# A layer norm moved to ScalarE, wider stores, eleven gather slots and a re-written order in a state-space and expert-lookup kernel

## The chip, the cores and the metric

The kernel runs on one core of one Trainium2 chip. The metric is the device time of one execution in microseconds; a verdict compares medians of several executions of the kernel before and the kernel after.

## What is computed

The reference takes 2048 tokens of 448 channels, normalises each token, and adds three things: the token itself, a long convolution along the sequence (branch A), and a lookup of experts (branch B).

```python
x = A_u
xn = _layernorm(x, axis=-1)
return x + _A_ref(xn, ...) + _B_ref(xn, ...)

# A: a state-space convolution per channel d, 256 states n, 2048 lags l
P = jnp.exp(logdA[:, :, None] * l[None, None, :])        # complex
K = jnp.einsum("dn,dnl,dn->dl", Cc, P, dB).real
y = irfft(rfft(pad(u)) * rfft(pad(K)))[:L] + u * Dskip

# B: 16 heads, best of 64 x 64 experts by two argmaxes
s1 = jnp.einsum("nhd,ed->nhe", q1, k1)
s2 = jnp.einsum("nhd,ed->nhe", q2, k2)
act = _gelu(jnp.einsum("nd,nhkd->nhk", xf, u[top_e]))
out = jnp.einsum("nhk,nhk,nhkd->nd", g, act, v[top_e])
```

## The kernel before

The work is written as some 3,400 small steps in 77 streams. Each step has an engine, a function that issues its instructions, the steps it depends on, and the buffers that it takes and gives back. A string, `ORDER`, holds one character for each step; the loop in `Plan.run` walks it and issues the steps. The order in which instructions stand on each engine is therefore fixed by that string; the costs that stand in the `p.add` calls are only notes of the program that wrote it and act on nothing. Synchronisation follows from the buffers: an instruction waits by a semaphore for the last reader or writer of what it touches. Each engine takes its instructions strictly in order, and so does the queue of loads and stores that SyncE issues (SP). The kernel also gives GpSimd (POOL) a queue of its own for gathers and for stores that add to memory.

The steps that the change and the prediction touch are these.

- **Layer norm** (`ln`, L895 on). Sixteen tiles `xx` of 128 tokens are loaded (L892) and normalised in pairs. VectorE (DVE) makes mean and variance of a tile with `bn_stats` (L909) and `bn_aggr` (L913), then ten small instructions a pair for the inverse root (L915 to L921), and ScalarE (ACT) applies scale and bias (L925) into the second half of the tile's buffer. The normalised tile goes to memory (`xn_d`, L929), to the transform of branch A (`up`, L724) and to the scores of branch B.
- **Scores** (`score`). TensorE (PE) multiplies the turned tile `xt` by combined weights `W` (L961, L970); DVE finds the maxima (L985, L992 and on). `W` is made at the start from the query weights `wq` (L855) and the keys (`wc`, L862) by PE and ACT.
- **Experts** (`experts`, L1062 on). For each tile of 128 tokens sixteen times: an indirect DMA on POOL gathers 128 rows of 3584 bytes into a slot `ue` (L1083), DVE takes the dot product of the first half of each row with the token's row `xr` (L1091, loaded at L1075), ACT and DVE make the weight, and PE adds up the second halves (`po`, L1121). PE's matmul gives four slots back. A finished tile is added to the output in memory by a POOL store with accumulation (L1136).
- **Convolution kernels** (`batch`, `products`). In 56 batches ACT makes exponentials and sines, DVE multiplies them (L660 to L666), PE turns them into the spectrum `VK` (L682, L702).
- **Convolution** (`conv`). The 448 channels go in chunks of 128, 128, 128 and 64. In each, four quarters are multiplied with the spectra (`U`, `cp`), turned back (`ip`, L825 and L830) and copied by ACT to `tq`. A store then puts `tq` to memory (`t_d`, L842) as rows of 128 (in the last chunk 64) numbers.
- **Last transform** (`final`). The stored quarters come back with another partition order (`tl`, L1166), PE multiplies them with the matrix `h` (L1178). In the first three chunks ACT copies the result and POOL adds it to the output in memory (L1192). The last chunk is written differently: `h` is loaded whole (`hb`, L1150), the output so far is read back into `bb` (L1156), DVE adds the two (L1182), and SP stores the sum (L1190).
- **Buffers**. One pool of 1024-number buffers holds the tiles `xx`, `W`, the gathered rows and most of the convolution's work. `OPT` gives 8 of them to gathered rows at the start; others join when the tiles, `W` and constants are used up.

Of the kernel before, what the change touches and what calls it, by code (L numbers as in the profile page):

```python
# [25 lines left out]
M = 2 * NB  # L26
# [89 lines left out]
class Plan:  # L116
# [57 lines left out]
    "44H444HH1HH2704HH7HH2HHH46HH7HH24444I6H4444H47H8CH22NI2H4241DE4HHC88142OC78D4D127H4H1EKECH74C44FLKF4CHHDL47HDEEFKDFFL24H"  # L174
    "27EC4J42HMF2HDC227KLI272223QEI47DC44E4346CDFFDK441C4QE4C9FDE978L88FDRQ9M4CREE94J74497J75RCKF5F8LQ4KCD977R71D4wE77E9778CL"
    "FFDEDAE6YFF7AYK9QHHLQANH7OQRHR9GR8S8AH9wQZH9HRaTwRHAQGHeRQYTHRQTHGQTRTRYHNHRHOSTQJTAQGMTHTeTHbQTRTTReTQUcQdQRVeNfRIVOWgg"
    "PXRQRfQPPPxBRRggHSxQTfgRxTyHeTRggIRZxTgwMXJxQKTyxHLyyfgQKLgzxQRh!!HRNRyyOz#xSPyyHQgzT!MH#QQxxggzgJTT$h!RyhTxRxR#HQRgfhgT"
    "#HQyTbghyh$yzQx!fHz!#NxyReOyiQ#TeHTHx$gyxRwYHeyxRTwxzQeUKHSeVQR!whgLhHwRjgHgcQQKQx!PRydzgY#yHRLHTbyIJRINHR#ThgThHx$bhHhH"
    "TOgKcLkRHVaTyMSdxgzxgT!!QiHxQzRyKHxQj#eHTyPTQRTyTHhxQfyTz!Hk#H%LggRRz$JhQMxH!iHjRRfhHRgxKg#TLHkyIfYhygTW#exyeTSexiX$KLYg"
    "lxKlLNMeyjzO!IHQzHgxKy!mygLPK#yTkTMxmQ#Hyl$ggwJQRHhzLRh!Thgmg!HezQfxhRex#gK#eQHwRwxThheHyxLgRgHR$y%QfggRHNxxOUiyjwfyzQ!z"  # L180
    "TMx!hy#byZSQggVVT#cQeHxyHRykHlgHHgzx$a!hRxJHgQ!gQHzTIYmhKTy&x#gLTh#digXIKTeQRyRTLJYP$fNjggTRhRlxOgeHyyHkHQzfKgh!gLxmzHHh"
# [21 lines left out]


class Kernel:
    OPT = dict(UE=8, XX=4, CS=2, ZI=2, MG=4, KT=4, HL=2, SG=1, XR=4, OB=3, XT=1, ST=1)
# [180 lines left out]
    def params(s, part):  # L387
# [874 lines left out]
```

## Time and profile before

| what | value |
|---|---|
| time before, median of 3 runs | 782.04 us (777.7 to 784.82) |
| the profiled execution, its own time | 777.9 us |
| its span, from first to last instruction | 776.1 us |
| mean granted TensorE clock | 0.908 |
| DVE busy | 680.7 us (88%) |
| PE busy | 658.5 us (85%) |
| ACT busy | 535.7 us (69%) |
| POOL busy | 351.3 us (45%) |
| moved by DMA | 212.36 MB, mean 274 GB/s |

The profile is of one execution. Busy time is the time in which an engine had an instruction running; shares are of the span. Views that group instructions give the count, the busy time and the mean of one instruction, then the idle time ahead of them and what ended it. A view by windows gives, for each stretch of time, busy time by engine, the clock granted to TensorE, the share of the 16 DMA engines that was busy, and GB/s.

### The profile page before, as it was taken

The page shows a single profiled execution, that of the slowest core. Times are in us where ns is not written, and L with a number is a line of the kernel's source. Part 1 is how long each engine was busy: PE and PEld are TensorE (multiplying, and loading weights), DVE is VectorE, ACT ScalarE, POOL GpSimd, SP SyncE. Part 2 cuts the span into 40 slices and gives each one's busy share as a digit, 9 for nine tenths or more (in the row PEclk, how much of TensorE's full clock was granted, in tenths as well). Part 3 has the DMA queues.
Part 4 walks back from the last instruction along what each step waited for, and adds up shares of the span by engine and source line. Part 5 has one row for each costly group of instructions (what it writes and reads, how often), then busy time and mean ns, then how long its engine had stood idle before and what let it go on. Part 6 is the DMA issues. An engine that isn't in the chain of part 4 may idle for free.

```text
span 776.1 us, 19859 instructions
## 1 busy us (share of the span) xinstructions
PE 658.5 (85%) x7628; PEld 358.9 (46%) x7628; DVE 680.7 (88%) x1727; ACT 535.7 (69%) x1071; POOL 351.3 (45%) x303
## 2 busy tenths in 40 slices
PE   1999999998999998999888967788995775899982
PEld 0434343443434344434356644456763442577751
DVE  5878659998999999999999999799998999999840
ACT  1756237457677597665668899698797998789720
POOL 2011033353623435557455474555466585744620
PEclk9999999999999999999899997566996767699995
DMA  9997956767867859778999999898898997999996
GB/s 310 355 331 287 318 163 209 261 197 243 273 205 222 260 174 310 235 239 265 319 338 329 314 345 306 271 254 269 257 315 286 348 302 237 345 296 293 274 264 125
DMA packets 139975, 212.36 MB, mean 274 GB/s; under 512 B 45096, under 2 KB 121896, under 8 KB 139816
## 3 DMA queue, kind: packets, MB, share of 16 engines
q0 software_dynamic: 29120, 124.27, 50.2%
q1 hardware_dynamic: 110760, 86.81, 36.8%
q8 instruction: 60, 0.98, 0.5%
q14 instruction: 35, 0.29, 0.1%
HBM read 181.42 MB, written 33.29 MB: 277 GB/s over the span
## 4 chain that ended last, share of the span: by engine, by line
DVE 30%; PE 29%; DMA 19%; ACT 12%; issue 7%; POOL 1%; SPq 1%; DVEq 0%; ACTq 0%; POOLq 0%
PE sc L961 10%; DMA ue<-in_uv_dram,ig 7%; DVE ue L1091 7%; DVE zi L662 3%; DVE ph L614 3%; DVE mg L666 3%; DMA xr<-xn_d 3%; PE wc L862 3%; PE kp L682 2%; PE sc L970 2%; ACT CS L629 2%; PE ip L830 2%; ACT CS L632 2%; DVE cp L808 2%; PE up L724 2%
## 5 line engine op out<-in xcount | busy, mean ns | idle before, releaser
L1083 POOL DMA_INDIRECT ue<-in_uv_dram,ig x256 | 307.3, 1200 | 334.4 <-PE po L1121 87.1
L961 PE MATMUL sc<-W,xt 128*128 128x512 f32 x384 | 181.4, 612 | 4.6 <-ACT xt L946 3.8
L1091 DVE SCALAR_TENSOR_TENSOR ue<-ue,xr 128x448 f32<-128x448 f32 x256 | 155.8, 619 | 17.4 <-DMA ue<-in_uv_dram,ig 11.6
L961 PEld LDWEIGHTS sc<-W,xt 128*128 128x128 f32 x384 | 69.7, 192 | 93.8 <-issue 82.7
L1121 PE MATMUL po<-ue,A 128*32 128x448 f32 x512 | 70.1, 616 | 10.2 <-issue 3.9
L682 PE MATMUL kp<-mg 128*32 128x64 f32 x1792 | 64.1, 240 | 14.9 <-DVE mg L666 6.5
L590 ACT ACTIVATE mg<-lg 128x512 f32<-128x512 f32 x112 | 63.2, 597 | 18.7 <-PE lg L579 17.9
L629 ACT ACTIVATE CS<-ph 128x1024 f32<-128x1024 int32 x56 | 62.7, 1120 | 8.0 <-DVE ph L614 5.4
L662 DVE TENSOR_TENSOR zi<-mg,CS 128x1024 f32<-128x1024 f32 x56 | 68.2, 1218 | 0.0
L666 DVE TENSOR_TENSOR mg<-mg,CS 128x1024 f32<-128x1024 f32 x56 | 68.2, 1217 | 0.0
L614 DVE CUSTOM_DVE_ANT_0 ph<-st,ph 128x512 uint16<-128x512 uint16 (+2 forms) x84 | 65.1, 775 | 0.3
L635 ACT ACTIVATE CS<-CS,halfpi 128x1024 f32<-128x1024 f32 x56 | 64.4, 1151 | 0.5
L682 PE MATMUL kp<-zi 128*32 128x64 f32 x1792 | 63.4, 238 | 0.0
L632 ACT ACTIVATE CS<-ph 128x1024 f32<-128x1024 int32 x56 | 63.1, 1127 | 0.1
L682 PEld LDWEIGHTS kp<-mg 128*32 128x32 f32 x1792 | 46.5, 121 | 35.3 <-issue 8.6
L702 PE MATMUL vp<-f,kt 128*64 128x128 f32 x448 | 42.0, 319 | 21.9 <-DVE kt L693 9.3
L985 DVE TENSOR_REDUCE mx<-sc 128x8 f32<-128x512 f32 x64 | 43.7, 683 | 14.5 <-PE sc L970 10.8
L579 PE MATMUL lg<-lc,rt 32*128 32x512 f32 x112 | 40.4, 564 | 14.4 <-ACT mg L590 10.8
L682 PEld LDWEIGHTS kp<-zi 128*32 128x32 f32 x1792 | 48.8, 123 | 0.1
L702 PEld LDWEIGHTS vp<-f,kt 128*64 128x64 f32 x448 | 27.8, 156 | 45.3 <-DVE kt L693 9.0
L798 PE MATMUL U<-VU,g 128*64 128x128 f32 x384 | 42.2, 299 | 5.4 <-DVE cp L808 3.4
L830 PE MATMUL ip<-cp,e 64*128 64x256 f32 x384 | 45.4, 383 | 0.2 <-ACT tq L837 0.2
(246 smaller groups left out, 1221.3 us busy)
## 6 DMA issues: line engine op xcount, KB each, us to landing
wq<-in_wq_dram SPq DMA_DIRECT2D x32, 448.0 KB
xr<-xn_d SPq DMA_DIRECT2D x64, 224.0 KB
vu_d<-vst SPq DMA_DIRECT2D x64, 112.0 KB
VU<-vu_d SPq DMA_DIRECT2D x12, 512.0 KB
t_d<-tq SPq DMA_DIRECT2D x24, 256.0 KB
tl<-t_d SPq DMA_DIRECT2D x12, 512.0 KB
ue<-in_uv_dram,ig POOLq DMA_INDIRECT x256, 6.4
xx<-in_x_dram SPq DMA_DIRECT2D x16, 224.0 KB
```

The costliest lines, as they stand in the source:

```text
L614: s.nc.vector.tensor_tensor(out=rw(n, 2 * n), in0=rw(0, n), in1=o["st"][:, k, b0:b0 + 2].rearrange("p b h m x -> p (b h m x)")[:, None].to ...
L629: s.nc.scalar.activation(CS[:, 1].rearrange("p (m r x) -> p m r x", r=16, x=2), four(s.ph), AF.Sin, scale=SC)
L632: s.nc.scalar.activation(B["CS"][:, 0].rearrange("p (m r x) -> p m r x", r=16, x=2), four(s.ph), AF.Abs)
L635: s.nc.scalar.activation(B["CS"][:, 0], B["CS"][:, 0], AF.Sin, scale=-SC, bias=s.halfpi)
L662: V.tensor_tensor(out=zi[:, 512:], in0=mg[:, 512:], in1=CS[:, 1], op=ALU.mult)
L666: V.tensor_tensor(out=mg[:, 512:], in0=mg[:, 512:], in1=CS[:, 0], op=ALU.mult)
L682: s.nc.tensor.matmul(kp[32 * c:32 * c + 32, 64 * gi:64 * gi + 64], T[ri][:, 1024 + m:1056 + m], view(T[ri], m, [[512, 2], [1, 32]]), start ...
L702: s.nc.tensor.matmul(vp[64 * ri:64 * ri + 64, 128 * gi:128 * gi + 128], B["kt"][:, 64 * gi:64 * gi + 64], s.f1[:, ri], start=True, stop=True)
L961: s.nc.tensor.matmul(B["sc", q].rearrange("p a b -> p (a b)"), B["xt"][:, i], w, start=(q % 2 == 0 and i == 0), stop=(q % 2 == 1 and i == 2))
L1083: s.nc.gpsimd.indirect_dma_start(out=ue, out_offset=None, in_=s.io["uv"], in_offset=bass.IndirectOffsetOnAxis(ap=s.IDX[t][:, c, g:g + 1].b ...
L1091: s.nc.vector.scalar_tensor_tensor(Q["ue", c][:, :D], Q["ue", c][:, :D], 1.0, B["xr", c], op0=ALU.mult, op1=ALU.mult, accum_out=Q["dot"][: ...
L1121: s.nc.tensor.matmul(B["po"][32 * c:32 * c + 32, :D], Q["A"][:, c], Q["ue", c][:, D:], start=(g == 0), stop=(g == 3))
```

## The change

- **Layer norm by ScalarE.** `bn_stats` and `bn_aggr` go. For each tile ACT runs two passes with an accumulated output: a copy scaled by -1/448, whose sum is minus the mean (new L907), and a square with that as bias, whose sum is the variance times 448 (new L911). The bias is then a plain product on DVE. The two passes write to the half of the buffer that L925 fills later.
- **Stores of turned rows.** `t_d` becomes one tensor for each chunk, laid out so that a partition of `tq` is one run of 4096 bytes (2048 in the last chunk) in place of eight runs of 512 (256).
- **Weight and parameter loads.** `wq` and the six parameter arrays are laid out on the host so that each partition reads one run of 3584 bytes in place of two of 1792.
- **Slots.** `OPT` gives 11 buffers to gathered rows in place of 8. The memory for them comes from the descriptor memory of POOL's DMAs: `dynamic_dma_scratch_size=4096` is set, which was left at its default.
- **Last chunk of the output.** It is written as the other chunks are: `h` in quarters beside each `tl`, a copy by ACT, and an accumulating store by POOL. The whole `h`, the read-back `bb`, the DVE addition and the SP store go.
- **Another `ORDER`.** All rows of the string differ, so nearly every engine's rows differ.

```diff
-    "44H444HH1HH2704HH7HH2HHH46HH7HH24444I6H4444H47H8CH22NI2H4241DE4HHC88142OC78D4D127H4H1EKECH74C44FLKF4CHHDL47HDEEFKDFFL24H"
...
+    "4HH4HH44441444Z4444H606HH414144114H72III2II72II2I2I7728I8I2IJJ22I2I2I2I72KIZ414I82852I24K4I4COP224C4234LMLDHMHHH4LMDCLM4"
...
-    OPT = dict(UE=8, XX=4, CS=2, ZI=2, MG=4, KT=4, HL=2, SG=1, XR=4, OB=3, XT=1, ST=1)
+    OPT = dict(UE=11, XX=4, CS=2, ZI=2, MG=4, KT=4, HL=2, SG=1, XR=4, OB=3, XT=1, ST=1)
...
-        s.t_d = dr.tile([64, 2, 32, D], F32, name="t_d")
+        s.t_d = [dr.tile([64, 2, 32, w], F32, name="t_d%d" % i) for i, (d0, w) in enumerate(s.chunks)]
...
-                s.nc.sync.dma_start(B[n], io[n].rearrange("(t p) d -> p t d", p=128))
+                s.nc.sync.dma_start(B[n], io[n])
...
-                    s.nc.sync.dma_start(s.t_d[:, ri, 8 * q:8 * q + 8, d0:d0 + w],
-                                        Q["tq"][64 * ri:64 * ri + 64].rearrange("p k h d -> p (k h) d"))
+                    s.nc.sync.dma_start(s.t_d[ck][:, ri, 8 * q:8 * q + 8].rearrange("p k d -> p (k d)"),
+                                        Q["tq"][64 * ri:64 * ri + 64].rearrange("p k h d -> p (k h d)"))
...
-                s.nc.sync.dma_start(B["w", sd], s.io["wq"][h, sd].rearrange("t p d -> p t d"))
+                s.nc.sync.dma_start(B["w", sd], s.io["wq"][h, sd])
...
-                s.nc.vector.bn_stats(B["bs"][:, i], s.XN[t][:, 0])
+                s.nc.scalar.activation(s.XN[t][:, 1], s.XN[t][:, 0], AF.Copy, scale=-1.0 / D, accum_out=B["m"][:, i:i + 1])
             return f
+
+        def sq(i, t):
+            return lambda: s.nc.scalar.activation(s.XN[t][:, 1], s.XN[t][:, 0], AF.Square, bias=B["m"][:, i:i + 1], accum_out=B["s"][:, i:i + 1])
...
-        ops = [(80, lambda i=i: s.nc.vector.bn_aggr(B["mv"][:, i], B["bs"][:, i])) for i in range(n)]
-
-        ops.append((73, lambda: s.nc.vector.tensor_scalar(B["v"], B["mv"][:, :, 1], 1e-5, None, op0=ALU.add)))
+            v = p.chain("ln_s", "ACT", [(ac(D) + 190, st(i, t)), (ac(D) + 280, sq(i, t))], deps=[ld[i]] + ([v] if i else []),
+                        take=("lnt",) if i == 0 else ())
+        ops = [(73, lambda: s.nc.vector.tensor_scalar(B["v"], B["s"], 1.0 / D, 1e-5, op0=ALU.mult, op1=ALU.add))]
...
-        ops.append((73, lambda: s.nc.vector.scalar_tensor_tensor(B["q"], B["mv"][:, :, 0], -1.0, B["y"], op0=ALU.mult, op1=ALU.mult)))
+        ops.append((73, lambda: s.nc.vector.tensor_mul(B["q"], B["m"], B["y"])))
...
-                    s.nc.vector.tensor_tensor(out=H["b"][:, 4 * g:4 * g + 4], in0=B["po"], in1=H["b"][:, 4 * g:4 * g + 4], op=ALU.add)
...
-                    s.nc.sync.dma_start(o, H["b"][:, 4 * g:4 * g + 4])
...
+                s.nc.scalar.activation(B["ob"], B["po"], AF.Copy)
...
+                s.nc.gpsimd.dma_start(o, B["ob"], accum_op=ALU.add)
...
-    nc = bacc.Bacc("TRN2", target_bir_lowering=False, num_devices=1)
+    nc = bacc.Bacc("TRN2", target_bir_lowering=False, num_devices=1, dynamic_dma_scratch_size=4096)
```

How the instructions stand, at the two places that matter most. First, DVE in the middle of the layer norms, where the fifth pair of tiles is normalised among dot products, score maxima and products of the convolution kernels. Before:

```order
L1091 SCALAR_TENSOR_TENSOR ue,dot<-ue,xr 128x448
L921 SCALAR_TENSOR_TENSOR q<-mv,y 128x2
L992 TENSOR_TENSOR eq<-sc,mx 128x512
L909 BN_STATS bst<-xx 128x6
L1000 TENSOR_TENSOR eq<-eq,wt 128x2048
L1091 SCALAR_TENSOR_TENSOR ue,dot<-ue,xr 128x448
L985 TENSOR_REDUCE mx<-sc 128x8
```

With the change, DVE starts such a pair at L915, and ACT has two rows for each tile, here the pair's second, among its exponentials (`mg`) and the copy of the turned tile (`xt`) for which PE's scores wait:

```order
L614 ISA ph<-st,ph 128x512
L915 TENSOR_SCALAR v<-s 128x2
L1107 SCALAR_TENSOR_TENSOR th<-th,dw 128x4
L1114 TENSOR_TENSOR A<-mask,th 128x128
L1091 SCALAR_TENSOR_TENSOR ue,dot<-ue,xr 128x448
L916 TENSOR_SCALAR y<-v 128x2
```

```order
L590 ACT_TABLE_LOAD
L590 ACTIVATE mg<-lg 128x2x256
L1041 ACTIVATE exg<-top 128x32
L907 ACTIVATE xx,m<-xx 128x448
L911 ACTIVATE xx,s<-xx,m 128x448
L590 ACTIVATE mg<-lg 128x2x256
L946 ACTIVATE xt<-xtp 128x512
```

The two large rows of a pair on DVE are gone, and ACT has four rows more for each pair, in line with its other work.

Second, the end of the SP queue, where the last chunk's quarters are stored (`t_d`) and come back (`tl`). Before:

```order
L1169 DMA hl<-in_h_dram 128x256
L842 DMA t_d<-tq 64x8x64 x4
L1166 DMA tl<-t_d 128x8x64 x3
L1156 DMA bb<-out_dram 128x4x64
L1166 DMA tl<-t_d 128x8x64
L1190 DMA out_dram<-bb 128x4x64 x4
```

With the change; the last two rows stand there four times:

```order
L1149 DMA tl<-t_d_84 128x8x128
L1151 DMA hl<-in_h_dram 128x256
L842 DMA t_d_85<-tq 64x512 x6
L1149 DMA tl<-t_d_85 128x8x64
L1151 DMA hl<-in_h_dram 128x256
```

And POOL's last rows with the change, where the last row stood on SP before:

```order
L1083 DMA ue<-in_uv_dram,ig 128x896 x19
L1136 DMA out_dram<-ob 128x448
L1167 DMA out_dram<-tl 128x4x128 x3
L1136 DMA out_dram<-ob 128x448
L1167 DMA out_dram<-tl 128x4x128
L1167 DMA out_dram<-tl 128x4x64 x4
```

Each `tl` of the last chunk now has its own part of `h` behind it in the queue, and the four stores of the last chunk went from SP to POOL.

More of the change, by code (lines that the diff above doesn't have):

```diff
@@ L178 @@
[L178 to L181, printed above, removed]
@@ L205 @@
+    "!r!ttsu)$r%+#!tts$tt#(*%+,)$u$%,,&uu)*(+,*+)*,))**+++,,,")
 class Kernel:
[L206 removed]
+    OPT = dict(UE=11, XX=4, CS=2, ZI=2, MG=4, KT=4, HL=2, SG=1, XR=4, OB=3, XT=1, ST=1)
     def __init__(s, tc, es, io, **opt):
@@ L1143, in final @@
         d0, w = s.chunks[ck]
-        last = ck == len(s.chunks) - 1
-        H = {}
-        if last:
-            def lh():
-                H["h"] = s.flat("q", "hb", 1024).rearrange("p (x e) -> p x e", e=32)
-                s.nc.sync.dma_start(H["h"], s.io["h"])
-            def lb(g):
-                def f():
-                    if g == 0:
-                        H["b"] = s.flat("q", "bb", 1024).rearrange("p (t d) -> p t d", d=w)
-                    s.nc.sync.dma_start(H["b"][:, 4 * g:4 * g + 4], s.io["out"][4 * g:4 * g + 4, :, d0:].rearrange("t p d -> p t d"))
-                return f
-            h = p.add("g_h", "SP", xf(128, 4096), lh, take=("ue",), deps=[s.VKlast])
-            base = [p.add("g_b", "SP", xf(512, 4 * w), lb(g), take=("ue",) if g == 0 else (), deps=[s.part[t] for t in range(4 * g, 4 * g + 4)])
-                    for g in range(4)]
         for g in range(4):
@@ L1165, in l1 @@
                 B["tl"] = s.flat("q", "tl", 8 * w).rearrange("p (x d) -> p x d", x=8)
[L1166 to L1169 removed]
+                s.nc.sync.dma_start(B["tl"], s.t_d[ck].rearrange("(x c) r k d -> x (c r k) d", c=2)[8 * g:8 * g + 8].rearrange("x p d -> p x d"))
+                B["h"] = s.flat("hl", "hl", 256).rearrange("p (x e) -> p x e", e=32)
+                s.nc.sync.dma_start(B["h"], s.io["h"][:, 8 * g:8 * g + 8])
             def m(B=B, g=g):
@@ L1196, in final @@
-            a = p.add("g_p" if last else "f_p", "PE", 8.0 * w if last else 1000, m, deps=[a], take=("kv",), give=("ue",) if last else hs)
-            if last:
-                a = p.add("g_v", "DVE", dv(4 * w), v, port=False, deps=[a, base[g]], give=("kv",))
-                p.add("g_st", "SP", xf(512, 4 * w), st, deps=[a])
-            else:
-                a = p.add("f_a", "ACT", ac(4 * w), v, deps=[a], give=("kv",))
-                s.fin[ck, g] = p.add("f_st", "POOLQ", 2 * xf(512, 4 * w), lat=4000, hold=1400, fn=st, deps=[a, s.res[g]], take=("og%d" % g,),
-                                     give=("og%d" % g, "ue"))
+                s.nc.gpsimd.dma_start(o, B["ob"], accum_op=ALU.add)
@@ L1205, in plan @@
+            a = p.add("f_l1", "SP", xf(1024, 4 * w) + xf(128, 1024), l1, n=2, deps=[s.t_done[ck]], take=("ue", "hl"))
+            a = p.add("f_p", "PE", 1000, m, deps=[a], take=("kv",), give=("hl",))
+            a = p.add("f_a", "ACT", ac(4 * w), v, deps=[a], give=("kv",))
+            p.add("f_st", "POOLQ", 2 * xf(512, 4 * w), lat=4000, hold=1400, fn=st, deps=[a, s.res[g]], take=("og%d" % g,),
+                  give=("og%d" % g, "ue"))
     def plan(s):
```

78 lines of the change are left out of this document (32 added, 46 removed).

## The prediction

> **What bounds the kernel now.** I read the busy times first, then the chain of work that ended last, then a view by windows, then what DVE waited for. The page's busy times say that two engines are nearly full, and the chain gives them equal shares:
>
> ```profile
> PE 658.5 (85%) x7628; PEld 358.9 (46%) x7628; DVE 680.7 (88%) x1727; ACT 535.7 (69%) x1071; POOL 351.3 (45%) x303
> DVE 30%; PE 29%; DMA 19%; ACT 12%; issue 7%; POOL 1%; SPq 1%; DVEq 0%; ACTq 0%; POOLq 0%
> ```
>
> An average over the span doesn't tell which of them to relieve, so I cut the span. In the view by windows the columns are the length, then busy time of PE, PEld, DVE, ACT and POOL with instruction counts, granted clock, DMA share and GB/s:
>
> ```profile
> 0.00:17.00 17.00, 0.44 (x1) 0.29 (x2) 8.64 (x18) 1.28 (x1) 5.75 (x17) 1.00 0.90 300
> 17.00:145.00 128.00, 123.17 (x505) 50.99 (x504) 101.28 (x219) 68.66 (x163) 25.23 (x20) 1.00 0.82 279
> 145.00:391.00 246.00, 231.70 (x1799) 99.77 (x1797) 234.37 (x642) 166.01 (x352) 115.06 (x97) 0.99 0.78 247
> 391.00:727.00 336.00, 272.78 (x4653) 185.24 (x4654) 318.35 (x797) 288.89 (x525) 195.00 (x162) 0.83 0.96 299
> 727.00:762.00 35.00, 26.06 (x552) 19.16 (x548) 16.39 (x50) 10.83 (x31) 9.14 (x9) 0.91 0.97 236
> 762.00:776.00 14.00, 4.31 (x128) 3.47 (x128) 1.70 (x4) 0.00 (x0) 1.15 (x1) 0.50 0.78 142
> ```
>
> Five stages are to be seen. Up to 17 us the first weights arrive. To 145 us PE is 96% busy and DVE only 79%: PE bounds. To 391 us both are at 94 to 95%. To 727 us DVE is at 95% and PE at 81%, with the DMA engines at 96%: DVE bounds, with the gathers close behind. The last 49 us are a tail of stores, loads and a few matmuls. So from 145 to 727 us DVE has 552.7 us of work in 582 us, 29.3 us of it idle, and that is the stretch to argue about. What ended DVE's idle time there, longest first (us in total, times, longest):
>
> ```profile
> DVE ue L1091 <- DMA ue<-in_uv_dram,ig: 10.8, 12, 2.4
> DVE ue L1091 <- DMA xr<-xn_d: 5.6, 4, 3.6
> DVE x L1101 <- ACT x L1098: 3.0, 5, 1.2
> ```
>
> More than half of it, 16.4 us, was waiting for data of the experts; the rest are short stops for ACT and PE.
>
> **The layer norm.** Its rows, and the rows nearest to what ACT now does:
>
> ```profile
> L909 DVE BATCH_NORM_STATS2 bst<-xx 128x6 f32<-128x448 f32 x16 | 9.7, 619 | 3.8 <-DMA xx<-in_x_dram 3.8
> L913 DVE BATCH_NORM_AGGREGATE mv<-bst 128x2 f32<-128x6 f32 x16 | 2.6, 172 | 0.0
> L727 ACT ACTIVATE vst<-up 128x448 f32<-128x448 f32 x32 | 17.5, 547 | 15.6 <-PE up L724 14.9 <-issue 0.6
> L925 ACT ACTIVATE xx<-xx,q,y 128x448 f32<-128x448 f32 x16 | 11.9, 756 | 14.6 <-DVE q L921 14.6
> L1091 DVE DVE_READ_ACCUMULATOR ue<-ue,xr 128x1 f32 x256 | 20.9, 82 | 0.0
> L639 ACT ACTIVATE dum<-one 128x1 f32<-128x1 f32 x28 | 5.7, 203 | 0.3
> ...
> 117.14 0.62 DVE L909 BATCH_NORM_STATS2 bst<-xx 128x6 f32<-128x448 f32 x1
> ```
>
> DVE loses 0.619 + 0.172 = 0.79 us for each tile, 12.3 us for sixteen. The last row, from the timeline, is the eighth tile's statistics: eight tiles have theirs before 145 us, where PE bounds, and there I count nothing; the other eight stand among DVE's work in the full stretch: 8 x 0.79 = **-6.3 us** (bounds 0 and -12.3). ACT gains two passes for each tile. The one with constants is like L727, 0.55 us; the one with one operand pointer lies between L727 and L925, which has two, so 0.65 us. Reading an accumulator has no ACT row; DVE's takes 0.08 us, and ACT's own instruction on one number for each partition 0.20 us, so I take 0.14 us. That is 1.48 us a tile and 23.7 us in all, on an engine that is busy 68.7 of 128 us and 166.0 of 246 us in the stages where it falls. The cover is ACT's idle time of 59 and 80 us. It is not perfect, since ACT works in order: behind a pass stand the copy of the turned tile (L946), for which PE's scores wait, and exponentials. I take **+1 us**, with bounds of 0 and +20.
>
> **The gather slots.** POOL's longest wait, and the time from issue to landing of a gather:
>
> ```profile
> POOL ue L1083 <- PE po L1121: 87.1, 30, 11.3
> ue<-in_uv_dram,ig POOLq DMA_INDIRECT x256, 6.4
> ```
>
> POOL stood 87.1 us for slots that PE gives back. With three more slots the written order can put gathers further ahead: counted in the two orders, a gather stands 2.8 gathers ahead of its dot product on average before and 3.6 with the change. The 12 stops of DVE were 0.9 us each on average, and 0.8 of a gather more ahead is worth about 2 us, since in the full stretch a gather comes every 582 / 235 = 2.5 us, by this row of that stretch:
>
> ```profile
> L1083 POOL DMA_INDIRECT ue<-in_uv_dram,ig x235 | 283.3, 1206 | 271.8 <-PE po L1121 82.3 <-issue 47.2 <-PE ip L830 11.7
> ```
>
> I take two thirds of the 10.8 us, **-7 us**. The bounds are 0 (the order spends the slots elsewhere) and -16.4 (the token rows too arrive in time).
>
> **Stores and loads.** Of queue rows (packets, MB, share of the 16 engines), the first is the page's gathers, the second a stretch of 3 us at 427 us that is nearly all 512-byte pieces, the third 4 us at 751 us with many 256-byte pieces:
>
> ```profile
> q0 software_dynamic: 29120, 124.27, 50.2%
> ...
> q1 hardware_dynamic: 1584, 0.80, 96.2%
> ...
> q1 hardware_dynamic: 1833, 0.68, 71.0%
> ```
>
> A DMA engine moves 124.27 MB / (0.502 x 776 us x 16) = 19.9 bytes a ns in the large pieces and 17.3 in the 512-byte ones. The 6.3 MB of the first three chunks' stores then shrink from 22.7 to 19.7 us of all engines, and the last chunk's 1 MB (4096 pieces at about 25 ns over 16 engines, 6.3 us) to 3.3. Three of these six microseconds lie where DVE bounds and are part of the gathers' term; the other three fall in the tail, below. Runs of 3584 bytes for `wq` and the parameters: the opening loads in runs of 1792 already ran at 300 GB/s and 0.90, 20.8 bytes a ns for an engine, above the gathers with their 3584. I take **0** (bounds -2 and 0). In the SP queue one more token tile of 224 KB stands ahead of the first weights; at 300 GB/s this is **+0.7 us**, bounds 0 and +2.
>
> **The tail.** These are pieces of the chain and of the timeline; the last line is the spread of POOL's accumulating stores of L1192, from issue to landing:
>
> ```profile
> 753.06 8.74 DMA t_d<-tq
> 763.17 6.13 DMA tl<-t_d
> ...
> 767.16 5.85 SPq L1190 DMA_DIRECT2D out_dram<-bb x4
> ...
> 772.19 0.42 DVE L1182 TENSOR_TENSOR bb<-po,bb 128x256 f32<-128x256 f32 x1 [1.19 <-PE po L1178]
> ...
> DMA to landing us min/median/max: 7.0/7.2/7.4
> ```
>
> The last of the quarters was issued at 753.1 us and landed at 761.8; it stood in a row of stores of 256-byte pieces, of which the change takes some 3 us: -2.5. From the last addition at 772.6 us to the end at 776.1 a plain store took 3.5 us; an accumulating one takes 7.0: +3.5. The copy on ACT in place of DVE's addition is about as long. Each quarter's `h` now follows its load in the SP queue and there are two buffers for it, so the third waits for PE to have used the first, and the fourth quarter's load waits behind it in the queue: one load's issue and a part of its flight, +1. Together **+2 us**, bounds -3 and +6.
>
> **The rest of the order** can close or open the 12.9 us of DVE's idle time that have nothing to do with data; I take **0**, bounds -8 and +8.
>
> The sum: -6.3 + 1 - 7 + 0 + 0.7 + 2 + 0 = -9.6 us. Against the profiled execution's own 777.9 us (its span 776.1 and 1.8 around it) this gives 768.3 us. That execution was 4.1 us under the median of the runs, 782.04 us, so I forecast a median of **772.4 us**, 1.2% less.
>
> **Rivals.** *The relief buys nothing.* Where DVE bounds, the DMA engines are busy 96% of the time and the gathers' 117 MB stay; and where PE is at 94% it would hold the pace though DVE has less to do. The stops of 10.8 us against the 318.35 us of DVE's work speak against a bound by DMA. Without the terms of -6.3 and -7, +3.7 us remain: 781.6, a median of 785.7 us.
>
> *More comes than I count.* If all waiting for experts' data ends and the order closes 8 us of the rest: -16.4 in place of -7, and -8: 750.9, a median of 755 us. The three more slots speak for it; that two engines at 94% leave little to close speaks against it.
>
> *ACT's sums become the late ones.* Place: the passes L907 and L911 ahead of L946 and the exponentials. Price: before 145 us PE waits for the whole of the eight tiles' passes, 8 x 1.48 = +11.8; after it DVE waits for the other eight, +11.8 - 6.3; the gathers gain nothing; with +0.7 and +2 the sum is +20.0, a median of 802 us: slower. It decides when ACT has no free stretch of 1.5 us ahead of what PE or DVE wants. ACT's 54 and 67% speak against it, PE's stops for L946 of 3.8 us in the scores, in the row below, for it.
>
> ```profile
> L961 PE MATMUL sc<-W,xt 128*128 128x512 f32 x384 | 181.4, 612 | 4.6 <-ACT xt L946 3.8 <-ACT eq L996 0.7
> ```
>
> The Trainium skill, page "ScalarE: Activation LUTs", section "Rules for kernel authors", speaks for this rival: it gives adds and products to VectorE and not to ScalarE. By that rule the change pays 1.48 us of ACT for 0.79 us of DVE, and the time is the 802 us of this rival. The trace agrees on the prices, not on which of the two engines is short.
>
> *POOL runs out of descriptor memory*, and the slots don't do what they are for. If it let two gathers fly at once, 256 x 6.4 / 2 = 819 us of gathers would not fit in 582, and the time would pass 1000 us. The trace shows no such wait, and it cannot show one for the smaller memory. The Trainium skill, page "DMA: Bandwidth & Descriptors", sections "Terms" and "The descriptor swizzle", gives 16 bytes for a descriptor and nine for each engine in a transfer of 128 partitions; an estimate from that is 4096 / 16 / 9 = 28 gathers in flight, more than 11 slots ask for. No run here shows it.
>
> **How the numbers follow.** My forecast gets 0.52, with its own range of 764 to 781 us; the relief that buys nothing 0.23, more than I count 0.14, ACT's sums 0.08, descriptor memory 0.03. A measurement of this kernel tells about 1% from no change, which is 774.2 to 789.9 us. Of the forecast's chance 0.42 lies below that and 0.10 inside; with the second rival 0.56 are faster; with 0.21 of the first's, 0.31 are the same; 0.13 are slower, the first's other 0.02 among them. The range goes from 757 us, near the better case, to 790 us, which takes in the case of no relief; about 0.08 is left out below and 0.12 above.
>
> **What would show it.** DVE's busy time near 667 us and ACT's near 560; DVE's stops for gathers between 145 and 727 us down to some 4 us; PE's stops for L946 not above 8 us; the last `t_d` landing some 14 us earlier, near 748 us, and then 19 us, not 14, to the end. The forecast is wrong if DVE's idle time in the long stretch stays near 29 us, if PE takes over the bound after 391 us, or if POOL's gathers issue more slowly than 1.2 us each.

## The result, and the profile after

The changed kernel took 762.22 us, median of four runs (759.13 to 763.02), against 783.43 us for the kernel before (four runs, 777.7 to 788.04): a ratio of 0.9725, with a 95% interval of 0.9653 to 0.9797. The forecast was 772.4 us, in a range of 757 to 790. The profiled execution after took 763.02 us, its span 761.1 us; before it was 777.9 and 776.1.

Busy times and the chain on the page of the kernel after:

```profile
PE 652.1 (86%) x7628; PEld 355.8 (47%) x7628; DVE 669.5 (88%) x1691; ACT 552.9 (73%) x1137; POOL 360.7 (47%) x307
PE 41%; DVE 29%; ACT 14%; DMA 7%; issue 6%; SPq 1%; POOL 1%; POOLq 0%; DVEq 0%; ACTq 0%
```

DVE lost 11.2 us of work, ACT gained 17.2. In the chain the DMA engines fell from 19 to 7%, and PE rose from 29 to 41%: less of the chain is now a wait for data, and more of it is matmuls that run one behind the other. To see where the 15 us of span went, I cut the span at the same events: the last score product (391.0 us before, 375.6 after), the last copy of the spectrum (L706, 734.0 and 718.3), the last landing of `t_d` (762 and 741). Only the cuts at 17 and 145 us are fixed times, as in the forecast. Columns as in the forecast's windows. After:

```profile
17.00:145.00 128.00, 123.48 (x443) 49.23 (x442) 98.81 (x215) 75.46 (x187) 27.01 (x22) 1.00 0.80 277
145.00:375.60 230.60, 226.07 (x1831) 98.77 (x1831) 225.57 (x612) 165.20 (x367) 115.69 (x97) 0.99 0.81 269
375.60:718.30 342.70, 278.50 (x4882) 190.34 (x4886) 327.19 (x818) 297.58 (x544) 202.05 (x162) 0.85 0.94 297
718.30:741.00 22.70, 19.14 (x352) 13.74 (x344) 10.41 (x36) 6.35 (x19) 4.77 (x4) 1.00 0.92 197
741.00:761.10 20.10, 4.31 (x128) 3.43 (x128) 0.00 (x0) 1.54 (x4) 6.43 (x5) 0.50 0.86 130
```

Before, with the cuts that the forecast did not have:

```profile
391.00:734.00 343.00, 279.19 (x4857) 190.13 (x4856) 324.51 (x814) 293.60 (x537) 198.19 (x164) 0.83 0.96 299
734.00:762.00 28.00, 19.65 (x344) 14.27 (x344) 10.23 (x32) 6.12 (x19) 5.95 (x6) 0.88 0.98 224
```

Row against row: from 145 us to the last score product 246.0 became 230.6 us (-15.4), the long stage behind it stayed (343.0, 342.7), the stores at its end gained 5.3 us and the last loads and stores lost 6. So the whole gain lies ahead of the last score product. From 145 us up to it both engines were nearly full before, and both are fuller now: PE's idle time fell from 14.3 us (246 - 231.70) to 4.5, DVE's from 11.6 to 5.0, and DVE has 8.8 us less work there.

Over the two stages together DVE had 558.9 us of work in 589.0 us before, 30.1 us idle, and has 552.8 in 573.3 now, 20.5 idle. That is 6.1 us less work and 9.6 us less waiting. What ended its idle time there, after:

```profile
DVE x L1101 <- ACT x L1098: 4.6, 6, 2.7
DVE th L1107 <- ACT th L1104: 3.8, 5, 1.3
DVE cp L808 <- ACT us L803: 2.2, 2, 1.5
DVE ue L1091 <- DMA ue<-in_uv_dram,ig: 2.0, 2, 1.0
```

The waits for gathers fell from 10.8 to 2.0 us, those for token rows from 5.6 to nothing. The short stops for ACT's small functions, 3.0 us on the longest such row before, are now the longest three, 10.6 us. How far the waits for data fall differs from one execution to the next: in a later profile of the same changed kernel (third round below) the gathers' row is

```profile
DVE ue L1091 <- DMA ue<-in_uv_dram,ig: 6.5, 6, 2.8
```

which makes 6.5 us of waits for data in place of 16.4, not 2.0.

### The profile page after: what moved, and what is told of

It is laid out like the page before. It is cut to its first block, busy times and chain, and to the rows that moved or that the text cites. A ratio compares the mean times of both kernels' runs of the same rounds, so it can differ in the third digit from the quotient of the medians.

```text
span 761.1 us, 19861 instructions
## 1 busy us (share of the span) xinstructions
PE 652.1 (86%) x7628; PEld 355.8 (47%) x7628; DVE 669.5 (88%) x1691; ACT 552.9 (73%) x1137; POOL 360.7 (47%) x307
## 4 chain that ended last, share of the span: by engine, by line
PE 41%; DVE 29%; ACT 14%; DMA 7%; issue 6%; SPq 1%; POOL 1%; POOLq 0%; DVEq 0%; ACTq 0%
PE sc L961 14%; DVE ue L1091 6%; PE U L798 3%; PE po L1121 3%; DVE mg L666 3%; DVE zi L662 3%; DVE ph L614 3%; PE kp L682 3%; PE sc L970 3%; DMA ue<-in_uv_dram,ig 3%; PE ip L830 2%; PE wc L862 2%; PE up L724 2%; ACT CS L629 2%; DMA VU<-vu_d 2%
## 5 line engine op out<-in xcount | busy, mean ns | idle before, releaser
L1083 POOL DMA_INDIRECT ue<-in_uv_dram,ig x256 | 312.6, 1221 | 309.0 <-PE po L1121 72.9
L1091 DVE SCALAR_TENSOR_TENSOR ue<-ue,xr 128x448 f32<-128x448 f32 x256 | 154.1, 617 | 4.0 <-DMA ue<-in_uv_dram,ig 4.0
L590 ACT ACTIVATE mg<-lg 128x512 f32<-128x512 f32 x112 | 63.4, 600 | 11.1 <-PE lg L579 10.6
L682 PE MATMUL kp<-mg 128*32 128x64 f32 x1792 | 62.3, 237 | 7.9 <-DVE kt L693 3.1
L682 PE MATMUL kp<-zi 128*32 128x64 f32 x1792 | 61.6, 234 | 0.0
L682 PEld LDWEIGHTS kp<-mg 128*32 128x32 f32 x1792 | 45.2, 119 | 29.2 <-issue 11.7
L702 PE MATMUL vp<-f,kt 128*64 128x128 f32 x448 | 43.6, 326 | 16.5 <-ACT tl L1163 5.0
L682 PEld LDWEIGHTS kp<-zi 128*32 128x32 f32 x1792 | 47.2, 121 | 0.1
L862 PE MATMUL wc<-wq,kk 128*64 128x448 f32 x128 | 31.7, 586 | 17.1 <-DMA wq<-in_wq_dram 17.1
```

The lines of the kernel that those rows point to most:

```text
L682: s.nc.tensor.matmul(kp[32 * c:32 * c + 32, 64 * gi:64 * gi + 64], T[ri][:, 1024 + m:1056 + m], view(T[ri], m, [[512, 2], [1, 32]]), start ...
L702: s.nc.tensor.matmul(vp[64 * ri:64 * ri + 64, 128 * gi:128 * gi + 128], B["kt"][:, 64 * gi:64 * gi + 64], s.f1[:, ri], start=True, stop=True)
L1083: s.nc.gpsimd.indirect_dma_start(out=ue, out_offset=None, in_=s.io["uv"], in_offset=bass.IndirectOffsetOnAxis(ap=s.IDX[t][:, c, g:g + 1].b ...
L1091: s.nc.vector.scalar_tensor_tensor(Q["ue", c][:, :D], Q["ue", c][:, :D], 1.0, B["xr", c], op0=ALU.mult, op1=ALU.mult, accum_out=Q["dot"][: ...
```

## The experiments

Twelve runs of eight kernels were made in four rounds, each beside runs of the kernel before on the same chip. On the chips of the first two rounds the kernel before itself took 833 and 826.5 us, on those of the last two 782 and 780; all 46 runs of the kernel before on the first two chips took between 812 and 843 us. Each round fell on another chip, so a trait of the chip can't be told from one of the occasion; "slower chip" below stands for either. Ratios are to the kernel before of the same round.

### First round: parts and order taken apart, on a slower chip

Edit of the first kernel, against the changed one: only the string, put in the order of the kernel before (each new step where the one that it replaces stood).

```diff
-    "4HH4HH44441444Z4444H606HH414144114H72III2II72II2I2I7728I8I2IJJ22I2I2I2I72KIZ414I82852I24K4I4COP224C4234LMLDHMHHH4LMDCLM4"
+    "44HH444HH1I2704II7II2III46II7II24444J6HH4444HH478C22OJ2I4241DE4IIC88142PC78D4D127I4I1ELECI74C44FMLF4CIIDM47IDEEFLDFFM24I"
...
```

> All parts of the change (layer norm sums on ScalarE, wide stores and loads, 11 slots, last chunk accumulated in memory), but the steps written in the order of the kernel before; where a step has another form now, its new form stands in the old step's place. If the relief of VectorE and the free slots carry the gain (my forecast's reason), most of it is here already: about 768 us, and VectorE's waits for gathers fall as they did with the change. If the written order carries it, this stays near the kernel before, 776 to 786 us, and TensorE's idle time between 145 us and the last score product stays near 14 us.

Second kernel, the layer norm's sums on DVE in the changed kernel:

```diff
-                s.nc.scalar.activation(s.XN[t][:, 1], s.XN[t][:, 0], AF.Copy, scale=-1.0 / D, accum_out=B["m"][:, i:i + 1])
+                s.nc.vector.bn_stats(B["bs"][:, i], s.XN[t][:, 0])
...
+        ops = [(80, lambda i=i: s.nc.vector.bn_aggr(B["mv"][:, i], B["bs"][:, i])) for i in range(n)]
```

> The changed kernel and its order, with only the layer norm's statistics back on VectorE (bn_stats and bn_aggr, where the ScalarE passes stood). If the 6.3 us that VectorE lost behind 145 us were on the path, as I forecast, this takes 6 to 9 us more than the changed kernel, 768 to 771 us. If the gain is the order's, VectorE absorbs them: 762 to 764 us. If ScalarE's passes cost something on the path, it is faster than the changed kernel.

Third, the old form of the last chunk in the changed kernel:

```diff
+                H["h"] = s.flat("q", "hb", 1024).rearrange("p (x e) -> p x e", e=32)
+                s.nc.sync.dma_start(H["h"], s.io["h"])
...
+                    s.nc.vector.tensor_tensor(out=H["b"][:, 4 * g:4 * g + 4], in0=B["po"], in1=H["b"][:, 4 * g:4 * g + 4], op=ALU.add)
...
+                    s.nc.sync.dma_start(o, H["b"][:, 4 * g:4 * g + 4])
```

> The changed kernel with the last chunk of the output written as before: h whole, the output read back, an addition on VectorE, a plain store by SyncE. The stretch from the landing of the last t_d store to the end was 14.3 us before and 20.2 us with the change; if that part of the change cost 6 us as the traces suggest, this is 756 to 757 us. If the read-back of the output takes the time back (its loads sit in the same queue), 760 to 763 us.

Fourth, the kernel before with 11 slots:

```diff
-    OPT = dict(UE=8, XX=4, CS=2, ZI=2, MG=4, KT=4, HL=2, SG=1, XR=4, OB=3, XT=1, ST=1)
+    OPT = dict(UE=11, XX=4, CS=2, ZI=2, MG=4, KT=4, HL=2, SG=1, XR=4, OB=3, XT=1, ST=1)
...
+    nc = bacc.Bacc("TRN2", target_bir_lowering=False, num_devices=1, dynamic_dma_scratch_size=4096)
```

> The kernel before in its own order, with 11 slots and the smaller descriptor memory. If slots shorten the waits for gathers by themselves, VectorE's 10.8 us of such waits between 145 and 727 us fall and the time is 774 to 778 us. If slots only help when the order puts gathers further ahead, the issue of gathers and the time stay: 780 to 786 us. If the smaller descriptor memory hinders POOL, gathers issue more slowly than 1.2 us each and it is slower than 786 us.

Measured, beside 833.13 us: parts in the old order 848.4 us (ratio 1.0178, 1.0118 to 1.0238), layer norm on DVE 850.69 (1.0165, 1.0099 to 1.0232), old last chunk 846.12 (1.0172, 1.0108 to 1.0236), the kernel before with 11 slots 833.09. The three that hold parts of the change were all slower than the kernel before, by the same 1.7%, which no theory had. They don't tell the parts apart, and none of them could be set against the changed kernel, which had not run there. Only the fourth gave an answer: with the old order, three more slots and the smaller descriptor memory show no effect on this chip, either way.

### Second round: the changed kernel itself on a slower chip

The first kernel is the changed one, with no edit.

> The changed kernel once more, unaltered, because the first four variants ran where the kernel before took 833 us and not 783, and all that held the change's parts came out 1.7% slower than before, where the change itself had been 2.75% faster. If the gain is a property of the two kernels alone, the ratio to the kernel before is again 0.97, wherever before itself lands (near 760 beside 783, near 808 beside 833). If the gain hangs on what limits the execution, then beside a kernel before of 833 us the changed kernel is at 840 to 850, a ratio of 1.01 to 1.02, and TensorE shows stops in the spectrum's matmuls (L682) for which nothing in the program is to blame, 25 us of them or more, where the first profile had under 1 us.

The second is the kernel before with the changed one's order and the 11 slots of the fourth kernel's edit; the steps that the change replaced stand where their successors stood.

```diff
-    "44H444HH1HH2704HH7HH2HHH46HH7HH24444I6H4444H47H8CH22NI2H4241DE4HHC88142OC78D4D127H4H1EKECH74C44FLKF4CHHDL47HDEEFKDFFL24H"
+    "4H4H44441444Z4444606H414144114H72IIIII2II72II2I2I7728I8I2IJJ22III2I2I2I72KIZ414I82852I24K4I4COP224C4234LMLDMHH4LMDCLM4D3"
...
```

> The kernel before with only the written order of the changed one: layer norm sums on VectorE, 512-byte stores, loads in runs of 1792, the old last chunk; 11 slots, since the new order needs them. Forecast's theory (relief of VectorE and slack of the gathers; the slots come with the order here): 6.3 us for the layer norm and some 3 us for the stores are lost against the changed kernel, so about 1.2% slower than it, half way to the kernel before. Rival (the written order carries the gain): within 0.5% of the changed kernel.

The third is the first kernel of the first round again.

> All parts of the change in the written order of the kernel before, again, now beside the changed kernel itself. Forecast's theory: the layer norm's 6.3 us and the stores' 3 us are kept, the 7 us of the gathers are not, since the old order leads each gather by 2.8 and not 3.6: 0.9 to 1.2% slower than the changed kernel and as much faster than before. Rival (order): as slow as the kernel before or slower, 2.5 to 3% above the changed kernel.

The fourth loads `h` whole for the last chunk and keeps the accumulating stores:

```diff
+            def lh():
+                H["h"] = s.flat("q", "hb", 1024).rearrange("p (x e) -> p x e", e=32)
+                s.nc.sync.dma_start(H["h"], s.io["h"])
+            h = p.add("g_h", "SP", xf(128, 4096), lh, take=("ue",), deps=[s.VKlast])
```

> The changed kernel with the last chunk's matrix h loaded whole ahead, as in the kernel before, and the accumulating stores kept: no part of h stands between the last loads in the SP queue, and no load waits for TensorE to give back a buffer of h. The changed kernel's tail from the last landing of t_d to the end took 20.2 us against 14.3 before. Theory that the two small buffers of h cost it: TensorE's waits for h (12.6 us) go, the four loads are issued in a row, and the end comes 3 to 5 us earlier (0.4 to 0.6%). Rival, that the accumulating store and the loads' own flight set the tail: less than 1 us.

Measured, beside 826.55 us: the changed kernel 833.05 us (1.0055, 1.0007 to 1.0103), old parts in the new order 843.53 (1.0172, 1.0109 to 1.0234), new parts in the old order 838.1 (1.0056, 1.0001 to 1.0110), whole `h` 832.95 (1.0070, 1.0026 to 1.0114). The same change that gave 2.75% gave nothing here. That lies between the two halves of the first expectation: the stops of PE are there, as its second half had it, but the ratio is below the 1.01 to 1.02 named with them. The old parts in the new order were 10.5 us slower than the changed kernel, so the parts are worth 1.2% in that order on this chip too. The order is worth nothing here: with the old parts it costs 1.7%, with the new ones the two orders come out alike. (The new parts in the old order were at 1.0178 in the first round: the slower chips differ by 1.2% among themselves for one and the same kernel.)

The windows show how the orders come out alike. The new parts in the old order, then the changed kernel, each from 145 us to the last score product and from there to the last L706:

```profile
145.00:415.10 270.10, 244.78 (x1850) 105.39 (x1841) 232.38 (x639) 176.30 (x386) 108.70 (x98) 0.96 0.73 230
415.10:790.70 375.60, 298.27 (x4856) 198.16 (x4856) 325.04 (x814) 294.11 (x537) 190.63 (x162) 0.83 0.86 269
```

```profile
145.00:397.40 252.40, 236.89 (x1830) 102.52 (x1831) 226.28 (x612) 165.25 (x367) 114.45 (x97) 0.97 0.76 248
397.40:791.70 394.30, 309.27 (x4883) 205.70 (x4886) 328.62 (x818) 298.02 (x544) 201.29 (x162) 0.81 0.85 259
```

The new order gains 17.7 us up to the last score product and loses 18.7 behind it. The long stage takes 376 to 394 us here, where it took 343 in the first pair, with the same instructions and nearly the same work of DVE and ACT. What is new in it against the first pair, among PE's waits within that stage and in the timeline, both of the changed kernel on this chip (start, length, engine, line, instruction, idle time ahead):

```profile
PE kp L682 <- issue: 19.1, 47, 1.2
...
463.96 0.23 PE L682 MATMUL kp<-mg 128*32 128x64 f32 x1 [0.44 <-issue]
...
464.67 0.33 PE L682 MATMUL kp<-zi 128*32 128x64 f32 x5 [0.43 <-issue]
465.40 0.27 PE L682 MATMUL kp<-zi 128*32 128x64 f32 x2 [0.40 <-issue]
466.14 0.98 PE L1121 MATMUL po<-ue,A 128*32 128x448 f32 x2 [0.46 <-issue]
```

In this excerpt PE stops every 0.73 us for some 0.43 us, and the profile names nothing that it waited for; in the first pair's profiles the row has 0.3 us before and is missing after. PE's busy time in the stage is 309.3 us too, where it was 278.5 in the first pair. With the 19.1 us of stops that makes 50 us of the 64 that PE had idle there (342.7 - 278.5). DVE waits longer for ACT at the same time: in this stage 19.6 us at L693 and 17.9 at L1101, where the first pair's profile after has 0.9 and 4.6.

The stops are not the new order's own. Over the whole execution L682 has 26.8 us of them here, 24.7 with the new parts in the old order, and 24.8 in the kernel before with 11 slots. But in the old order the two waits of DVE are shorter, 9.0 and 12.6 us, and DVE is idle for 50.6 us of the stage (375.60 - 325.04) in place of 65.7. So under about the same stops the new order loses more; that the stops are the reason, and how, was argued from these rows and not tried.

The whole `h` settled its own question. PE's waits in the tail, first the changed kernel on this chip, then the kernel with whole `h`:

```profile
PE po L1159 <- DMA hl<-in_h_dram: 9.5, 3, 7.1
```

```profile
PE po L1167 <- DMA tl<-t_d: 7.5, 2, 6.2
PE po L1167 <- DMA hl<-in_h_dram: 1.7, 2, 1.2
```

The wait for `h` goes and one for `tl` takes its place; from the last `ip` matmul to the end it is 23.8 us with the quarters and 23.0 with the whole. The two small buffers cost under 1 us; by these rows the flight of the loads and POOL's stores set the tail.

### Third round: a chip like that of the first pair

The changed kernel, unaltered:

> The changed kernel, unaltered, as the base of the two runs beside it. If the kernel before is again near 830 us, the ratio is within 1.00 and 1.01 as in the second round of runs; if it is near 783 us, 0.97. Either way the stage from 17 us to the last score product should be some 15 us shorter than that of the kernel before with 11 slots (395.7 us where that ran), and what the ratio lacks should be missing from the stage after it.

The changed kernel with its own order up to the last score product and the old one behind it; here the first row that differs, the fourteenth of the string:

```diff
-    "h!hyfURRjnhTiRkhhS$U#hyS$y%UiymjUzilk!#UlxV$$xg%&hzzz!zzWh#!(Sn#hRSyyzyiz!iyyRmRS#V#$Wh!my$$inno$fUoyfigSSph%hzfgp%zfzUq"
+    "h!hyfURRjnhTiRkhhS$U#hyS$y%UiymjUzilk!#UlxV$$xg%&hzzz!zzWh#!(Sn#hRSyyzyiz!iyyRmRVWXhffgfhUUimionihngYp#YSh$UhS#$p!f$iSh$"
...
```

> All parts of the change; the changed kernel's written order up to the last score product, and from there on the old order for all steps that are left. The profiles so far say that the new order gains 15 us up to the last score product and, where TensorE has stops of its own in the spectrum's matmuls, loses 11 to 15 us behind it, by waits of VectorE for ScalarE (rows L693 and L1101, 37 us together). Theory that these waits come from how the new order interleaves the later stage: 8 to 15 us faster than the changed kernel (0.985 to 0.99 of it) and faster than the kernel before wherever it runs. Rival, that the later stage is longer because work was only pushed behind the last score product: within 0.5% of the changed kernel.

The layer norm on DVE, as in the first round:

> The changed kernel with the layer norm's sums on VectorE again (bn_stats and bn_aggr), at the same places of the written order, all else as changed. The forecast's term for it is 6.3 us, bounds 0 and 12.3: so 0.8% slower than the changed kernel by the forecast's theory. Rival, that TensorE and not VectorE sets the pace up to the last score product, so that VectorE's relief is worth nothing by itself: within 0.3% of it, and then the stores and the last chunk carry the 10.5 us by which the old parts in the new order were slower.

Measured, beside 782.04 us: changed 767.95 us (0.9787, 0.9725 to 0.9849), new order followed by the old 768.31 (0.9830, 0.9779 to 0.9882), layer norm on DVE 771.19 (0.9860, 0.9810 to 0.9910). The gain is back beside a kernel before of 782 us. The layer norm's relief is worth 3.2 us by the medians and 5.7 by the ratios (0.73% of 782); the intervals overlap, so these times alone do not show that it is worth anything. The traces below say more. The order of the later stage is worth nothing, which these rows show, from the changed kernel and from the one of two orders:

```profile
145.00:377.70 232.70, 228.49 (x1844) 99.82 (x1844) 227.77 (x619) 166.46 (x370) 116.93 (x98) 0.99 0.82 270
377.70:725.70 348.00, 275.39 (x4882) 187.29 (x4886) 326.97 (x818) 298.15 (x544) 218.21 (x162) 0.86 0.94 293
```

```profile
145.00:378.00 233.00, 228.68 (x1848) 99.72 (x1846) 227.95 (x614) 166.31 (x368) 117.20 (x98) 0.99 0.82 268
378.00:725.80 347.80, 283.53 (x4887) 194.64 (x4886) 328.16 (x826) 298.86 (x546) 202.12 (x162) 0.83 0.94 294
```

348.0 and 347.8 us, with either order: DVE is busy for 94% of that stage in both. The kernel of two orders was made to win back what the new order loses on the slower chips; whether it does was not tried, since this round fell on another chip. No version tried beats the changed kernel here.

### Fourth round: the order alone, again

> The kernel before with only the written order of the changed one and its 11 slots, once more: layer norm sums on VectorE, 512-byte stores, loads in runs of 1792, the old last chunk. Beside a kernel before of about 782 us the changed kernel came out at 0.979 and with the layer norm's sums back on VectorE at 0.986. If the parts carry the gain, this kernel is at 0.99 to 1.00; if the written order with its slots carries it, at 0.975 to 0.985. The forecast's terms give 0.99 (the gathers' 7 us are kept, the layer norm's 6.3 and the stores' 3 are lost). Beside a kernel before of about 830 us it should repeat the 1.017 measured there, and would then say nothing new on the other condition.

This is the second kernel of the second round, unaltered. Measured: 774.58 us beside 779.74 (0.9925, 0.9885 to 0.9965), where the forecast's terms gave 0.99. The interval does not touch the changed kernel's of the third round. The stage up to the last score product, and the one behind it; then the first of these two of the third round's kernel with the layer norm on DVE:

```profile
145.00:383.30 238.30, 230.05 (x1850) 99.94 (x1848) 235.23 (x642) 159.48 (x346) 116.52 (x99) 0.99 0.82 268
383.30:729.50 346.20, 279.48 (x4883) 191.30 (x4886) 326.05 (x816) 297.74 (x544) 207.14 (x162) 0.84 0.95 292
...
145.00:384.90 239.90, 231.77 (x1860) 100.87 (x1860) 236.98 (x649) 161.94 (x350) 118.58 (x101) 1.00 0.83 268
```

238.3 us: about half way from the kernel before (246.0) to the changed one (230.6, and 232.7 in the third round). Of the time as a whole the order with its slots gives about a third, 0.75% or 5.9 us, and the parts the rest, 1.4%.

Put side by side, these traces tell the parts apart up to the last score product. It ends at 391.0 us in the kernel before. In the new order with the layer norm on DVE it ends at 383.3 (all parts old) and 384.9 (all other parts new), and with the layer norm on ACT at 375.6, 377.7 and 378.0. So there the order with its slots is worth 6 to 8 us, the layer norm in that order 5 to 9, and the other parts nothing that shows. One profile stands for the kernel before, and the one that ends at 384.9 is of an execution 6.7 us above its kernel's median. The order alone already brought DVE's idle time in this stage from 11.6 to 3.1 us (238.30 - 235.23) and PE's from 14.3 to 8.2: DVE was then busy for 99% of it, and its work was what was left to take away.

## Why the prediction was right, point by point

**The sum of the long stretch held, its place only in half.** The forecast argued about DVE's stretch from 145 to 727 us, its 6.3 us of work and its waits for experts' data; with +1 for ACT its terms there make -12.3. Cut as above, that stretch lost 6.1 us of DVE's work and 9.6 us of its idle time, 15.7 us; all else together gave back 0.7. But all of it came ahead of the last score product, and most of the waits for data, 10.2 of 16.4 us, stood behind it, by these rows of the kernel before from 391 to 734 us:

```profile
DVE ue L1091 <- DMA ue<-in_uv_dram,ig: 6.4, 7, 2.4
DVE ue L1091 <- DMA xr<-xn_d: 3.8, 2, 3.6
```

After, 2.0 us of them are left there, and the stage takes 342.7 us for 343.0 all the same: DVE has 2.7 us more work in it and longer stops for ACT. For this stage the rival *the relief buys nothing* came true. It had named the DMA engines, busy for 96% of it (94% after); whether they hold the stage was not tried and stays open. And that DVE's work in the whole stretch fell by nearly the 6.3 us forecast is in part luck, since it is 8.8 us less in one stage and 2.7 more in the other.

**The layer norm, -6.3 us: right in size.** Up to the last score product it is worth 5 to 9 us by the traces, in the time 3.2 to 5.7 with intervals that overlap. ACT's passes, by the rows of the kernel after and, below the dots, the timeline of one tile and PE's row for L946:

```profile
L907 ACT ACTIVATE xx<-xx 128x448 f32<-128x448 f32 x16 | 9.3, 579 | 8.4 <-DMA xx<-in_x_dram 8.4
L911 ACT ACTIVATE xx<-xx,m 128x448 f32<-128x448 f32 x16 | 10.6, 664 | 0.3
L907 ACT ACTIVATION_READ_ACCUMULATOR xx<-xx 128x1 f32 x16 | 3.2, 203 | 0.0
L911 ACT ACTIVATION_READ_ACCUMULATOR xx<-xx,m 128x1 f32 x16 | 3.0, 188 | 0.0
...
102.48 0.56 ACT L907 ACTIVATE xx<-xx 128x448 f32<-128x448 f32 x1
103.74 0.19 ACT L911 ACTIVATION_READ_ACCUMULATOR xx<-xx,m 128x1 f32 x1
...
L961 PE MATMUL sc<-W,xt 128*128 128x512 f32 x384 | 180.1, 608 | 2.2 <-ACT xt L946 1.9
```

The four means sum to 0.579 + 0.664 + 0.203 + 0.188 = 1.63 us, but the rows overlap: from the start of the first pass to the end of the second reading a tile takes 1.45 us (102.48 to 103.93), where 1.48 was forecast, and ACT's busy time rose by 17.2 us in all, less than the 23.7 forecast. It was hidden, too: PE's stops for L946 fell to 1.9 us from 3.8, so the +1 was not needed; the longer stops of DVE at L1101 came with the order, 4.8 us of them in the fourth round with the sums on DVE. The rival *ACT's sums become the late ones* is refuted. The Trainium skill, page "ScalarE: Activation LUTs", section "Rules for kernel authors", gives adds and products to VectorE; here the sums on VectorE gave 0.9860 and those on ScalarE 0.9787, and the traces above have the same sign, since VectorE was the engine with no time left.

**The gather slots, -7 us: right in size, with another place, and the slots by themselves are nothing.** Waits for gathers and token rows fell by 14.4 us in the first pair and by 9.9 in the third round's profile; of the 14.4, some 5 came back as other stops. The order with its slots is worth 5.9 us in the fourth round, and by its trace they lie ahead of the last score product, where only 6.2 of the 16.4 us of waits for data stood. And 11 slots in the old order gave 833.09 beside 833.13, so without the order the slots bring nothing on that chip. Gathers issued in 1.18 us each there, so the rival *POOL runs out of descriptor memory* has nothing for it.

**Stores and loads, 0: too small, if anything; the weights, +0.7: about right.** Stores, loads and last chunk together make the step from 0.9925 to 0.9860, 5.1 us, though these two intervals overlap (0.9885 and 0.9910) and up to the last score product the two traces show no such step. The forecast had 0 for stores and loads, +0.7 for the weights and +2 for the tail. PE's waits for the first weights were 17.1 us, 16.6 before, so the +0.7 was about right. How much of the 5 us is stores, loads or last chunk was not tried apart on a chip like the first.

**The tail, +2: about right, by three errors that cancel.** The chain's last pieces after, and below the dots ACT's last copy from the timeline:

```profile
736.01 4.91 DMA t_d<-tq
741.06 2.89 DMA tl<-t_d
744.90 2.26 issue
747.21 1.25 POOL out_dram L1167
749.16 1.27 POOL out_dram L1167
750.43 3.72 issue
754.19 1.24 POOL out_dram L1167
755.99 1.31 POOLq L1227
...
755.21 0.38 ACT L1163 ACTIVATE tl<-po 128x256 f32<-128x256 f32 x1 [1.42 <-PE po L1159]
```

The last store's flight fell from 8.74 to 4.91 us; from its landing to the end it is 20.2 us (14.3 before; 19 was forecast). From the last L706 to that landing it is 22.6 us for 27.8, so the tail as a whole is 0.7 us longer. The stores gave 5.2 us where 2.5 was forecast. From the landing to the end of the last copy it is 14.7 us for 10.8, +3.9 where +1 was forecast: the fourth load of `tl` was issued at 746.82 us, 5.8 behind the first. From there to the end it is 5.5 us for 3.5, +2.0 where +3.5 was forecast, since the quickest of L1167's stores lands in 3.7 us and not in the 7.0 taken from larger ones. That the sum came out near +2 is luck. An `h` loaded whole gained under 1 us on the slower chip, so the +3.9 is not the buffers' of `h` alone.

**What was mis-sized.** The measured median lies 10 us below the forecast. Some 5 of these are in the traces: the profiled execution became 14.9 us shorter (777.9 to 763.0), not 9.6. The stretch from 145 us gave 3.4 us more than its terms, and all else cost 0.7 us where +0.7 and +2 were forecast. The other 5 are the base: the forecast put the median 4.1 us above the profiled execution, as it was before, but after the profiled execution was the slowest of the four, 0.8 above their median. In the third round, with more runs, the medians are 14.1 us apart (782.04 and 767.95), so a part of the 21 us of the first pair is scatter.

The rest of the order, put at 0 with bounds of 8, cost: DVE's idle time that has nothing to do with data rose from 13.7 us (30.1 - 16.4) to 18.5 (20.5 - 2.0), by stops for ACT. The rival *more comes than I count* had it falling by 8; it was right only in that nearly all waits for data went. And the forecast argued from DVE alone though both engines stood at 94 to 95%: PE's idle time up to the last score product fell from 14.3 to 4.5 us, which no term of it counts. On the slower chips the order and the parts pay only together there: the last score product ends at 412.7 us (kernel before with 11 slots), 415.1 (new parts, old order), 409.8 (old parts, new order) and 397.4 (both). On a chip like the first, the parts in the old order were not run.

**The rival *the relief buys nothing* on another chip.** Beside a kernel before of 826.55 us the changed kernel is at 1.0055: what the new order and the parts gain up to the last score product is lost again behind it. The forecast held that rival to depend on the DMA engines or on PE's pace. PE does have stops of its own there; that they are the cause was not shown.

Of the signs named beforehand: DVE's busy time 669.5 us (667 forecast), ACT's 552.9 (560), gathers' stops 2.0 (4), L946 1.9 (at most 8), the last landing of `t_d` at 740.9 (748), 20.2 us behind it (19). DVE's idle time in the long stretch is 20.5 us, not near 29. POOL's gathers issue in 1.221 us each and not in 1.200 (1.286 in the third round), which was named as a sign against the forecast; the gain came all the same.

## What to carry to other kernels

First close an engine's stops, then take work from it: in the new order DVE was busy for 99% of a stage, and there work moved away paid for itself, onto an engine with a third of its time free and at nearly twice the price (1.45 us for 0.79). Cut a stretch at events before forecasting over it: waits that end in a stage which does not get shorter are worth nothing. More buffers did nothing here until the order of issue used them. And a gain of 2 or 3% can vanish on another chip, so measure before and after side by side on more than one.

## What the runs showed of the hardware

The same kernel, the one before, takes 780 to 783 us on some chips and 827 to 833 on others, at nearly the same granted clock (0.91 and 0.89). On the slower two PE stops in runs of small matmuls (L682) for 25 to 44 us in 60 to 97 stops, by kernel, in the excerpt above some 0.43 us in every 0.73, with no releaser in the profile; on the others the row has at most 0.3 us. The row of the queue that carries instructions reads the same on both (of the third and the second round):

```profile
q8 instruction: 60, 0.98, 0.5%
```

The Trainium skill, page "Runtime: NRT & Kernel Launch", section "Instruction fetch mechanics", says that an engine's instructions are fetched in blocks of 16 KiB by a DMA queue of its own and that this is mostly hidden; 60 packets for 0.98 MB agree with the block's size. That the stops are late instructions is a guess that no run here tested; from 462 to 466.5 us, the stretch of the excerpt, this queue moved no packet at all, which speaks against it. Why two chips have the stops and others not stays open.

An accumulating pass on ACT has a row of its own of 0.19 to 0.20 us for reading the accumulator, where DVE's is 0.08; a part of it overlaps with its neighbours (a tile's two passes with their readings sum to 1.63 us and take 1.45).
